# Reading K and V in 32 KB reads, written in 1 KB pieces to two partitions, in a decode kernel

## The chip, the cores and the metric

The kernel runs on one core of one Trainium2 chip. The metric is the device time of one execution in microseconds (us). "Span" is the profile's time from the first instruction to the last of one profiled execution; it is 1.7 to 1.9 us shorter than the device time. HBM is the chip's main memory, SBUF the core's own, of 128 partitions. A "packet" is one entry in the trace's record of DMA transfers; in these kernels it is one contiguous read.

## The reference

One decode step for 8 sequences: attention over the last 2,048 positions of a key and a value cache, plus an MLP, mixed by a sigmoid gate.

```python
# x: 8 x 1 x 576; k_cache, v_cache: 8 x 16 x 8192 x 128 (bf16); 32 query heads, 16 key heads
W = min(4096, max(256, Sk // 4))                       # 2048
q = (x @ wq).reshape(B, Sq, Hq, Dh).transpose(0, 2, 1, 3)
k = jnp.repeat(k_cache[:, :, Sk - W:, :], rep, axis=1)
v = jnp.repeat(v_cache[:, :, Sk - W:, :], rep, axis=1)
p = _softmax(jnp.einsum("bhqd,bhkd->bhqk", q, k) * Dh ** -0.5)
a = jnp.einsum("bhqk,bhkd->bhqd", p, v).transpose(0, 2, 1, 3).reshape(B, Sq, Hq * Dh) @ wo
b = ...                                                # layernorm, gelu MLP with w1, w2
return g * a + (1 - g) * b
```

What matters here: 2 x 8 x 16 x 2,048 x 128 x 2 bytes = 134 MB of K and V have to come out of HBM, of 154 MB in all.

## The kernel before

K and V come in 64 loads of 2 MB. (In the code and the views below, `arena` is the SBUF memory that all buffers lie in, `SE` a slot's 8,192 elements in one partition, 16 KB, and `AST` the step from one partition to the next.) A load takes one key head and four batches. Each lands in one of nine slots of 16 KB in each of the 128 partitions: partition 4x + a holds keys 64x to 64x + 63 of batch a, which are 16 KB in one piece in HBM. So a load is 128 reads of 16 KB, each written as one piece into one partition.

```python
def src_of(cache, g, q):
    hkv, b0 = 2 * g + q // 2, 4 * (q % 2)
    return cache[b0:b0 + 4, hkv, S0:Sk, :].rearrange("a (x r) d -> x a (r d)", x=32)
# ... in k_unit(i), and alike in v_unit(i):
s = take_slot()
d = dma("sp", lambda e: e.dma_start(slot(s), src_of(A_k_cache, g, q)), "s%d" % s, ...)
# K: VectorE transposes the slot, TensorE multiplies it with the queries; V: TensorE reads the slot
```

Another load matters to the argument: wo (four chunks of 1.2 MB) already goes through a helper that tells the DMA an order of writing of its own. It reads 4,608 bytes at a time and writes them in four pieces of 1,152 bytes into four neighbouring partitions.

```python
def run_dma(nc, e, out, in_, shape=None):       # shape: row pitch and (step, count) pairs, outermost first
    ...
# wo_chunk(i):
src = bass.AP(A_wo.tensor, offset=128 * h0 * D, ap=[[4 * D, 32], [128 * D, WO_CH], [1, 4 * D]])
run_dma(nc, e, dst[:, :, 0:D], src, (AST, ((4 * AST, 32), (WOP, WO_CH), (AST, 4), (1, D))))
```

All these loads are issued from the SP queue (SyncE's). The profile counts their packets together as q1, and their time as a share of the span of 16 DMA engines. That share is 98.6% in before, so the 16 are about equally loaded; the argument takes it that each load is spread evenly over them, gives each a queue of its own and numbers these e = 0 to 15.

## Time and profile before

| | before |
|---|---|
| time, median of 2 runs | 369.19 us (369.14 to 369.24) |
| span of the profiled run | 367.5 us |
| DMA packets' time, share of 16 engines' span | 98.6% |
| TensorE, VectorE busy | 69%, 57% |

First, three rows of the page of before: how busy the 16 DMA engines are in 40 equal slices of the span (9 is 90% or more), what they moved, and the queue that moves nearly all of it (packets, megabytes, share of 16 engines' span).

```profile
DMA  8999999999999999999999999999999999999994
GB/s 345 428 408 428 428 427 433 432 426 432 435 430 432 422 427 430 432 439 431 426 430 428 422 438 427 430 426 428 433 430 430 428 431 426 433 428 432 418 424 191
...
q1 hardware_dynamic: 11776, 154.29, 98.6%
```

The DMA engines are busy for 98.6% of the span, so the kernel's time is, within 5 us, the sum of its packets' times on one engine. That says what bounds it. The chain of waits of before agrees (shares of the span by what ended last):

```profile
DMA 74%; DVE 12%; PE 11%; SPq 1%; ACT 1%; issue 1%; DVEq 0%; ACTq 0%
```

The list of DMA issues shows how far ahead the loads are asked for (count, KB, median us from issue to landing). One load takes about 4.9 us, so some seven are waiting at any time.

```profile
arena<-in_A_k_cache_dram SPq DMA_DIRECT2D x32, 2048.0 KB, 35.8
arena<-in_A_v_cache_dram SPq DMA_DIRECT2D x32, 2048.0 KB, 36.7
```

Two stretches of the steady part (from the windows view of before: start and end, length, busy time and count for PE, PEld, DVE, ACT and POOL, granted TensorE clock, DMA share, GB/s; a share of 1.00 or 1.01 is full):

```profile
165.00:200.00 35.00, 24.01 (x152) 7.30 (x113) 24.32 (x27) 5.55 (x14) 3.79 (x18) 0.87 1.01 433
230.00:260.00 30.00, 20.32 (x117) 5.49 (x86) 20.72 (x26) 4.95 (x13) 1.89 (x9) 0.79 1.01 433
```

Since packets are everything here, the trace's record of each packet (size, start, duration) is the finest ruler. Counted over before, on queue q1 (its smaller packets, and 128 each of 3,456 and 4,096 bytes, left out):

```
bytes read   packets   median ns   what
     2,304       128          93   w2
     4,608     1,280         178   w1, wo (1,024 of them), w2
    10,368       384         389   w2
    16,384     8,192         611   K, V      (8,083 of them exactly 611)
    32,768       128       1,213   wq
    36,864       128       1,364   w1
```

A packet here is one read; how many pieces it is written in doesn't show in its count. The busy times of the engines and the durations of the 32 K-load issues on the SP queue (shortest, median and longest in ns, then first and last start in us):

```profile
PE 254.8 (69%) x1815; PEld 87.3 (24%) x1429; DVE 210.1 (57%) x253; ACT 47.8 (13%) x117; POOL 37.6 (10%) x163
L645 SPq DMA_DIRECT2D arena<-in_A_k_cache_dram x32: 534/535/1442, 2.6 to 282.9; - x32
```

### The profile page before, as it was taken

Reading aid. Unit: us, or ns where it says so; the run is one execution under the profiler, and the core shown is the slowest. Engines: PE = TensorE matmul, PEld = TensorE weight load, DVE = VectorE, ACT = ScalarE, POOL = GpSimd, SP = SyncE. Lnnn points to the kernel's source line nnn. Section 1 sums busy time; section 2 is a strip of 40 time slices with the busy share of each in tenths; the row PEclk is TensorE's granted clock in tenths of the full one; section 3 lists DMA queues with packets and bytes.
Section 4 is the critical chain, followed back from the end, with each engine's and each line's share of the span. In section 5 each row is a group of like instructions: output and inputs, shape, how many; then the busy total and the mean of one; then the engine's idle time right before and its main releaser. Section 6 shows DMA issues by size and latency. Waiting matters only on the chain.

```text
span 367.5 us, 4111 instructions
## 1 busy us (share of the span) xinstructions
PE 254.8 (69%) x1815; PEld 87.3 (24%) x1429; DVE 210.1 (57%) x253; ACT 47.8 (13%) x117; POOL 37.6 (10%) x163
## 2 busy tenths in 40 slices
PE   0349982895598398673986397765966396865995
PEld 0339200131123032010321032111311031214552
DVE  0704699797667754459654764478544864473000
ACT  1010002100300310003000300003100300003200
POOL 7020010011012001000101001010101000000000
PEclk9999998799689879887898879696988789795559
DMA  8999999999999999999999999999999999999994
GB/s 345 428 408 428 428 427 433 432 426 432 435 430 432 422 427 430 432 439 431 426 430 428 422 438 427 430 426 428 433 430 430 428 431 426 433 428 432 418 424 191
DMA packets 11851, 154.59 MB, mean 421 GB/s; under 512 B 1292, under 2 KB 1332, under 8 KB 3000
## 3 DMA queue, kind: packets, MB, share of 16 engines
q1 hardware_dynamic: 11776, 154.29, 98.6%
q8 instruction: 13, 0.21, 0.2%
q10 hardware_dynamic: 56, 0.03, 0.1%
q14 instruction: 6, 0.05, 0.0%
HBM read 154.31 MB, written 0.01 MB: 420 GB/s over the span
## 4 chain that ended last, share of the span: by engine, by line
DMA 74%; DVE 12%; PE 11%; SPq 1%; ACT 1%; issue 1%; DVEq 0%; ACTq 0%
DMA arena<-in_A_k_cache_dram 50%; DMA arena<-in_B_w_dram 15%; DMA arena<-in_A_v_cache_dram 9%; DVE arena L660 9%; PE ps L173 5%; PE ps L516 2%; PE ps L677 1%; DVE arena L605 1%; PE ps L700 1%; SPq L765 1%; ACT arena L619 1%; DVE arena L624 1%; PE ps L518 1%; PE ps L715 1%; DVE arena L614 0%
## 5 line engine op out<-in xcount | busy, mean ns | idle before, releaser
L660 DVE STREAM_TRANSPOSE arena<-arena 128x2048 f32<-128x2048 f32 x64 | 145.2, 2297 | 78.9 <-DMA arena<-in_A_k_cache_dram 71.5
L173 PE MATMUL ps<-arena 128*128 128x512 bf16 x401 | 134.4, 445 | 15.3 <-DVE arena L660 9.8
L677 PE MATMUL ps<-arena 128*128 128x512 bf16 x115 | 51.8, 450 | 16.7 <-DVE arena L660 16.6
L709 ACT ACTIVATE arena<-ps 128x512 f32<-128x512 f32 x32 | 19.1, 598 | 196.7 <-PE ps L700 196.7
L677 PEld LDWEIGHTS ps<-arena 128*128 128x128 bf16 x128 | 14.6, 114 | 125.8 <-issue 66.8
L715 PE MATMUL ps<-arena 128*128 128x8 f32 x256 | 36.9, 275 | 8.7 <-ACT arena L709 7.7
L653 POOL COPY arena<-arena 32x32 bf16<-32x32 bf16 x128 | 26.0, 203 | 159.2 <-PE ps L173 144.6
L715 PEld LDWEIGHTS ps<-arena 128*128 128x128 f32 x256 | 35.6, 217 | 22.4 <-ACT arena L709 16.4
L700 PE MATMUL ps<-arena 128*32 128x512 bf16 x512 | 36.7, 413 | 6.0 <-DMA arena<-in_A_v_cache_dram 6.0
L669 PE MATMUL ps<-arena 128*128 128x512 bf16 x6 | 3.5, 585 | 37.8 <-DVE arena L624 37.8
L605 DVE TENSOR_REDUCE arena<-ps 128x1 f32<-128x2048 f32 x8 | 18.3, 2282 | 15.5 <-PE ps L173 15.5
L619 ACT ACTIVATE arena<-ps,arena 128x512 bf16<-128x512 f32 x32 | 21.6, 686 | 41.4 <-DVE arena L614 41.4
L700 PEld LDWEIGHTS ps<-arena 128*32 128x32 bf16 x512 | 11.3, 100 | 39.8 <-issue 24.1
L624 DVE STREAM_TRANSPOSE arena<-arena 128x512 bf16<-128x512 bf16 x32 | 19.8, 674 | 0.9 <-ACT arena L619 0.9
L733 POOL TENSOR_TENSOR arena<-arena 128x16 bf16<-128x16 f32 x15 | 4.0, 267 | 142.3 <-ACT arena L725 142.3
L516 PE MATMUL ps<-arena 128*128 128x8 bf16 x144 | 10.9, 201 | 4.5 <-DMA arena<-in_B_w_dram 4.5
L559 PE MATMUL ps<-arena 128*8 128x288 bf16 (+1 forms) x140 | 11.6, 315 | 1.9 <-DMA arena<-in_B_w_dram 1.7
L516 PEld LDWEIGHTS ps<-arena 128*128 128x128 bf16 x144 | 10.8, 159 | 5.0 <-DMA arena<-in_B_w_dram 5.0
L669 PEld LDWEIGHTS ps<-arena 128*128 128x128 bf16 x8 | 0.9, 107 | 45.1 <-DVE arena L624 45.1
L733 DVE TENSOR_TENSOR arena<-ps,arena 128x16 bf16<-128x16 f32 x1 | 0.2, 229 | 19.4 <-PE ps L715 19.4
L438 PE MATMUL ps<-arena 8*128 8x8 bf16 x8 | 0.5, 168 | 13.5 <-DVE arena L411 9.8
L631 DVE RECIPROCAL arena<-ps 128x32 f32<-128x32 f32 x8 | 2.9, 358 | 10.5 <-PE ps L629 10.5
(83 smaller groups left out, 95.6 us busy)
## 6 DMA issues: line engine op xcount, KB each, us to landing
arena<-in_A_k_cache_dram SPq DMA_DIRECT2D x32, 2048.0 KB, 35.8
arena<-in_A_v_cache_dram SPq DMA_DIRECT2D x32, 2048.0 KB, 36.7
arena<-in_B_w_dram SPq DMA_DIRECT2D x1, 4608.0 KB, 24.3
arena<-in_A_wq_dram SPq DMA_DIRECT2D x1, 4096.0 KB, 13.1
arena<-in_B_w_dram SPq DMA_DIRECT2D x3, 1296.0 KB, 33.9
arena<-in_B_w_dram SPq DMA_DIRECT2D x2, 576.0 KB, 28.7
arena<-in_A_wq_dram SPq DMA_DIRECT2D x1, 512.0 KB, 3.7
arena<-in_B_w_dram SPq DMA_DIRECT2D x1, 432.0 KB, 30.4
```

What stands on the lines that cost most here:

```text
L173: return e.add_instruction(mybir.InstMatmult(name=nc.get_next_instruction_name(), engine=mybir.EngineType.PE, ins=[e.lower_ap(rhs), e.lowe ...
L516: ins = e.matmul(out_, lhsT, yT[:, kt, :], start=(kt == 0), stop=False)
L559: ins = e.matmul(ps[32 * j:32 * j + 8, BK_ACC, 0:JN], lhsT, rhs[:, JN * j:JN * j + JN], start=False, stop=True, skip_group_check=True, til ...
L605: mx = add("dve", lambda e: e.tensor_reduce(out=k(MX), in_=ps[:, 0:4, :].rearrange("p a n -> p (a n)"), axis=AXL.X, op=ALU.max), deps=[qk_ ...
L619: return e.activation(out=Pm[:, 512 * c:512 * c + 512], in_=ps[:, c, :], func=ACTF.Exp, bias=k(NB), scale=SCALE, accum_out=k(SUM + c))
L624: pts.append(add("dve", (lambda c=c: lambda e: e.transpose(bass.AP(arena, offset=aoffs("PT") + 2048 * (g % 2) + 128 * c, ap=[[AST, 128], [ ...
L653: return e.tensor_copy(dst, src)
L660: tr = add("dve", (lambda h=h, kb=kb: lambda e: e.transpose(bass.AP(arena_f, offset=foffs("KT") + kb * 2048, ap=[[AST // 2, 128], [1, 2048]]),
L677: mm = e.matmul(*args, start=False, stop=last) if rc == 0 else held_matmul(nc, e, *args, stop=last)
L700: mm = e.matmul(ps[c:c + 32, BK_OS[i % 2], :], PT[:, g % 2, 512 * q + 32 * t:512 * q + 32 * t + 32], slot(s)[:, 512 * t:512 * t + 512], st ...
L709: u_ev[i] = add("act", lambda e: e.activation(out=EV[:, i % 2, :], in_=ps[:, BK_OS[i % 2], :], func=ACTF.Copy), deps=[prev] + ([u_sum[i - ...
L715: mm = e.matmul(ps[:, BK_S, OC + 16 * (item % 2) + 8 * (q % 2):OC + 16 * (item % 2) + 8 * (q % 2) + 8], EV[:, i % 2, 128 * r:128 * r + 128 ...
```

## The change

The intent is fewer and larger reads: 32 KB, which is 128 keys of one batch. A slot has only 16 KB in a partition, so a read has to be written into two partitions; the change takes two that are 64 apart and alternates between them every 1 KB. Key block e is four reads of 32 KB, one for each batch, written to partitions 4e to 4e + 3 and 64 + 4e to 64 + 4e + 3. (That is how the program lays the transfer out; the author counts block e as queue e's, but the trace doesn't name a packet's engine or partition.) Which keys lie in which partition changes, alike for K and V, so the result doesn't.

```diff
-        def src_of(cache, g, q):
+        def load_quad(e, cache, g, q, s):
             hkv, b0 = 2 * g + q // 2, 4 * (q % 2)
-            return cache[b0:b0 + 4, hkv, S0:Sk, :].rearrange("a (x r) d -> x a (r d)", x=32)
+            blk = 2 * 64 * Dh
+            src = bass.AP(cache.tensor, offset=((b0 * Hkv + hkv) * Sk + S0) * Dh, ap=[[blk, 16], [Hkv * Sk * Dh, 4], [1, blk]])
+            piece = 4 * Dh
+            dst = bass.AP(arena, offset=aoffs("RAW") + s * SE, ap=[[AST, 128], [piece, SE // piece], [1, piece]])
+            return run_dma(nc, e, dst, src, (AST, ((4 * AST, 16), (AST, 4), (piece, SE // piece), (64 * AST, 2), (1, piece))))
...
-            d = dma("sp", lambda e: e.dma_start(slot(s), src_of(A_k_cache, g, q)), "s%d" % s, 4 * W * Dh * 2, ...)
+            d = dma("sp", lambda e: load_quad(e, A_k_cache, g, q, s), "s%d" % s, 4 * W * Dh * 2, ...)
...    (the same for A_v_cache)
```

No other instruction moves: the order and the waits on the four compute engines are those of before, line for line.

More of the change, by code (lines that the diff above doesn't have):

```diff
@@ L644, in k_unit @@
             s = take_slot()
-            d = dma("sp", lambda e: e.dma_start(slot(s), src_of(A_k_cache, g, q)), "s%d" % s, 4 * W * Dh * 2, deps=slot_free[s], name="dk%d" % i, after=last_dma[-1:])
+            d = dma("sp", lambda e: load_quad(e, A_k_cache, g, q, s), "s%d" % s, 4 * W * Dh * 2, deps=slot_free[s], name="dk%d" % i, after=last_dma[-1:])
             last_dma.append(d)
@@ L692, in v_unit @@
             item = 2 * g + q // 2
-            d = dma("sp", lambda e: e.dma_start(slot(s), src_of(A_v_cache, g, q)), "s%d" % s, 4 * W * Dh * 2, deps=slot_free[s], name="dv%d" % i, after=last_dma[-1:])
+            d = dma("sp", lambda e: load_quad(e, A_v_cache, g, q, s), "s%d" % s, 4 * W * Dh * 2, deps=slot_free[s], name="dv%d" % i, after=last_dma[-1:])
             last_dma.append(d)
```

## The prediction

> **What bounds the kernel.** The DMA engines. The row of DMA shares over the span has them 90% busy or more in 38 of 40 slices; the queue list puts 98.6% of 16 engines' span on the one SP queue, at 421 GB/s over all and 428 to 432 GB/s in the steady stretches (windows view). TensorE is 69% busy and VectorE 57%. The chain of waits is 74% DMA. K and V loads are issued about 36 us before they land, so some seven are queued and the queue never runs dry. The packets' own time sets the kernel's.
>
> **What a packet costs.** The trace's packet records: 16,384 B takes 611 ns in 8,083 of the 8,192 K/V packets; 36,864 B takes 1,364 ns, 32,768 B 1,213 ns (median, wq), 4,608 B 178, 2,304 B 93. These lie on one line: about 8.6 ns a packet + 0.03677 ns a byte (27.2 GB/s an engine). The records count packets by the reading side. The wo load, which reads 4,608 B and writes it in four pieces of 1,152 B into four partitions, shows 178 ns too in two thirds of its packets, about 194 in the rest (mean about 183).
>
> **What the change does.** Each of 64 loads has 64 reads of 32 KB instead of 128 reads of 16 KB: 4 packets an engine at about 1,213 ns instead of 8 at 611, 4,852 against 4,888 ns. That saves 36 ns a load, 64 x 36 = 2.3 us for each engine, all on the critical path. It adds write pieces: 2,048 of 1 KB a load, 128 an engine. Issuing them should cost little: the wo load, 1,024 write pieces, holds the SP queue for 0.71 us, a K/V load for 0.54; I estimate under 1 us a load, one every 4.9 us. Instruction order, waits, bytes, slots and compute are unchanged.
>
> **The risk.** [...] wo's mean of 183 instead of 178 ns says that split writes may cost 2 to 3%. That much on K/V (1,213 to about 1,243 ns) would make a load 4,972 ns: +5.4 us instead of -2.3.
>
> **Prediction.** 369.2 - 2.3 = 366.9; with a little for contention 367.1 us, 8 in 10 within 365.6 to 373.5. Faster by over 2%: 0.02; within 2%: 0.85; slower by over 2%: 0.13.
>
> **What would show it.** q1 packets fall by 64 x 64 = 4,096 to about 7,680; K/V packets of 32 KB at 1,213 ns; steady rate 431 to 435 GB/s; DMA share about 98%; engines' busy times unchanged. Contention would show as K/V packets above 1,220 ns with DMA share still near 100% and a lower GB/s. Starvation would show as a DMA share below 95% and long SP issues.
>
> **What would make it wrong.** [...] a limit on queued pieces that holds back issue, or 16 engines reading 32 KB blocks colliding in memory (wq's first packets took up to 1.5 us).

The sum came to 369.2 - 2.3 = 366.9 us, and the 0.2 us "for contention" that makes it 367.1 was an estimate, for which no measured number was given. The +5.4 us of the risk is 64 loads of 4,972 - 4,888 = 84 ns.

## The result and the profile after

| | before | after |
|---|---|---|
| time, median of 2 runs | 369.19 us | 389.79 us (389.51 to 390.08) |
| ratio, 95% interval | | 1.0558 (1.0513 to 1.0604) |
| span | 367.5 us | 388.2 us |
| DMA share | 98.6% | 98.5% |
| K/V packets, median | 8,192 of 611 ns | 4,096 of 1,285 ns |
| a load on one DMA engine | 8 x 611 = 4,888 ns | 4 x 1,285 = 5,140 ns |

A ratio is the mean time of one kernel's fast runs over that of the other's in the same rounds, so it can differ a little from the ratio of the medians.

The same rows of the page of after:

```profile
DMA  8999999999999999999999999999999999999995
GB/s 337 456 403 410 397 419 396 419 397 419 409 400 422 358 413 395 419 396 416 414 395 419 375 400 398 415 407 382 409 409 407 384 393 410 409 405 409 376 417 216
...
q1 hardware_dynamic: 7680, 154.29, 98.5%
```

The packets fell by 4,096, as the prediction said, and the engines are as busy as before. They move less at the same busy share: 404 and 407 GB/s in the two stretches below, against 433. So the packets themselves got longer. The same two stretches in the windows view of after:

```profile
165.00:200.00 35.00, 24.03 (x137) 6.85 (x96) 24.12 (x27) 4.94 (x13) 2.96 (x14) 0.85 1.00 404
230.00:260.00 30.00, 21.57 (x126) 4.92 (x89) 13.75 (x7) 1.56 (x4) 3.16 (x15) 0.83 1.00 407
```

Summing the packet records of q1 and dividing by 16 engines says where the time went:

```
us for each DMA engine   before   after   difference
K and V                   313.4   331.2        +17.8
wo                         11.7    14.0         +2.3
everything else            37.4    37.3         -0.1
sum                       362.5   382.5        +20.0
span less sum               5.0     5.7         +0.7
span                      367.5   388.2        +20.7
```

Of the 17.8 us, 64 x (5,140 - 4,888) ns = 16.1 us is the longer ordinary packet, and the rest is packets above the ordinary length, most of them near the wo chunks.

Something else in the profile after catches the eye more. The chain of waits of after, and a piece of the SP queue's timeline (start us, length us, what):

```profile
SPq 39%; DMA 27%; PE 17%; DVE 14%; issue 2%; ACT 0%; DVEq 0%; ACTq 0%
```

```profile
145.54 4.64 SPq L193 DMA_DIRECT2D arena<-in_A_v_cache_dram  x1
150.63 4.63 SPq L193 DMA_DIRECT2D arena<-in_A_k_cache_dram  x1
155.72 4.63 SPq L193 DMA_DIRECT2D arena<-in_A_v_cache_dram  x1
```

The engines' busy times, the durations of the K-load issues, and the loads' times from issue to landing (last figure, us) in after:

```profile
PE 265.0 (68%) x1815; PEld 88.9 (23%) x1429; DVE 210.2 (54%) x253; ACT 47.7 (12%) x117; POOL 37.5 (10%) x163
L193 SPq DMA_DIRECT2D arena<-in_A_k_cache_dram x32: 800/4634/24121, 2.8 to 323.8; - x32
arena<-in_A_k_cache_dram SPq DMA_DIRECT2D x32, 1.0 KB, 14.9
arena<-in_A_v_cache_dram SPq DMA_DIRECT2D x32, 1.0 KB, 15.0
```

Issuing one load now takes 4.63 us, where the prediction estimated under 1 us, and the issues form 39% of the chain. That looks like a cause: as if writing out 2,048 pieces took the queue 4.6 us. It isn't. The first K load of the same run, with only the wq and w1 loads queued before it, was issued in 0.80 us, and the second was then held for 24.12 us, until 2.6 us after the first packet of K had started. That fits an issue that waits for room: fewer loads are under way at a time (landing 15 us after issue, not 36, at about 5.1 us a load), the SP queue stands in front of them, and the chain of waits passes through it. The DMA share of 98.5%, against 98.6% before, says that the engines themselves hardly waited for it. Nor does the SP queue's share of the chain follow the loss: in the runs below it is 16% at a loss of 17.6 us and 28% at 3.0 us. The chain names what was released last; which resource was full is told by the busy share.

### The profile page after: what moved, and what is told of

Read it like the earlier page. It is cut to its first block, busy times and chain, and to the rows that moved or that the text cites. A ratio compares the mean times of both kernels' runs of the same rounds, so it can differ in the third digit from the quotient of the medians.

```text
span 388.2 us, 4175 instructions
## 1 busy us (share of the span) xinstructions
PE 265.0 (68%) x1815; PEld 88.9 (23%) x1429; DVE 210.2 (54%) x253; ACT 47.7 (12%) x117; POOL 37.5 (10%) x163
## 3 DMA queue, kind: packets, MB, share of 16 engines
q1 hardware_dynamic: 7680, 154.29, 98.5%
## 4 chain that ended last, share of the span: by engine, by line
SPq 39%; DMA 27%; PE 17%; DVE 14%; issue 2%; ACT 0%; DVEq 0%; ACTq 0%
SPq L193 39%; DMA arena<-in_A_k_cache_dram 23%; PE ps L173 9%; DVE arena L664 7%; DMA arena<-in_B_w_dram 4%; DVE arena L609 4%; PE ps L719 3%; PE ps L681 3%; PE ps L704 2%; DVE arena L628 1%; DVE arena L618 1%; DVE arena L612 1%; PE ps L673 0%; SPq L769 0%; PE ps L633 0%
## 5 line engine op out<-in xcount | busy, mean ns | idle before, releaser
L173 PE MATMUL ps<-arena 128*128 128x512 bf16 x401 | 140.5, 463 | 15.6 <-DVE arena L664 11.1
L681 PE MATMUL ps<-arena 128*128 128x512 bf16 x115 | 53.4, 465 | 23.9 <-DVE arena L664 23.9
L704 PE MATMUL ps<-arena 128*32 128x512 bf16 x512 | 38.0, 424 | 8.9 <-DMA arena<-in_A_v_cache_dram 8.9
L673 PE MATMUL ps<-arena 128*128 128x512 bf16 x6 | 3.5, 585 | 37.8 <-DVE arena L628 37.8
L559 PE MATMUL ps<-arena 128*8 128x288 bf16 (+1 forms) x140 | 13.1, 343 | 1.6 <-DMA arena<-in_B_w_dram 1.5
```

Source lines behind the costliest of these rows:

```text
L173: return e.add_instruction(mybir.InstMatmult(name=nc.get_next_instruction_name(), engine=mybir.EngineType.PE, ins=[e.lower_ap(rhs), e.lowe ...
L681: mm = e.matmul(*args, start=False, stop=last) if rc == 0 else held_matmul(nc, e, *args, stop=last)
L704: mm = e.matmul(ps[c:c + 32, BK_OS[i % 2], :], PT[:, g % 2, 512 * q + 32 * t:512 * q + 32 * t + 32], slot(s)[:, 512 * t:512 * t + 512], st ...
```

## The experiments

The theories at the start:

- **Theory 1, the piece:** every further write piece of a packet costs something, wherever it goes. From after: (1,285 - 1,213) / 31 = 2.3 ns.
- **Theory 2, sharing:** pairs of queues now write through something that they share (the texts call it a port) and get in each other's way, the more so the longer each stays in one half of its partitions. That any two queues share such a thing no trace or run here shows.
- **Theory 3, the switch:** going from one partition to another costs something, 31 times a packet.

A fourth, that 32 KB reads are slow by themselves, has against it that wq reads 32 KB at 1,213 ns in both kernels. All experiments but the last change only the function `load_quad`, and all that ran to the end gave the right result. The diffs are cut to what differs: from the change in the first 1 KB run, in the runs of halves and in the 4 KB alternating run, from the first 1 KB run in the two runs after it, and from the two pieces of 16 KB in the run with pairs 4 apart. Times are beside runs of before on the same chip (369.14 and 369.22 us).

### 1 KB pieces in the loads of before

The reads of before, one partition to a read, but 16 pieces to a packet.

```diff
+            src = cache[b0:b0 + 4, hkv, S0:Sk, :].rearrange("a (x r) d -> x a (r d)", x=32)
             piece = 4 * Dh
+            return run_dma(nc, e, dst, src, (AST, ((AST, 128), (piece, SE // piece), (1, piece))))
```

> The loads of before (16 KB reads, each landing in one partition, 128 partitions), but written in 1 KB pieces: the pieces of the change without its pairs of partitions and without its 32 KB reads. Theory 1: 611 + 15 x 2.3 = 646 ns a packet, 8 x 646 = 5168 ns a load, time about 387 us. Theories 2 and 3: 611 ns, 369 us (if the queues keep the partitions that they had).

Measured: 386.77 us (386.63 to 386.85), ratio 1.0475 (1.0459 to 1.0491); K/V packets 645 ns (median). Theory 1 said 646 ns and 387 us. Most of the loss of the change is here, 17.6 of 20.6 us, without a 32 KB read, without a pair of partitions, and with the packet count of before. Theories 2 and 3 expected 611 ns and 369 us. The queue line, the chain of waits and the two stretches of this run:

```profile
q1 hardware_dynamic: 11776, 154.29, 98.8%
DMA 34%; PE 25%; DVE 23%; SPq 16%; issue 2%; ACT 0%; DVEq 0%; ACTq 0%
```

```profile
165.00:200.00 35.00, 24.05 (x130) 6.05 (x89) 24.20 (x27) 4.76 (x12) 2.93 (x14) 0.82 1.01 407
230.00:260.00 30.00, 20.58 (x127) 4.94 (x92) 15.19 (x7) 1.97 (x4) 3.51 (x17) 0.89 1.01 407
```

The engines are full with 11,776 packets and move 407 GB/s, just as with 7,680 packets after the change: it is the pieces that count, not the packets.

### 4 KB pieces in the loads of before

```diff
-            piece = 4 * Dh
+            piece = 16 * Dh
```

> The loads of before in 4 KB write pieces, 4 to a packet. Theory 1 (each further write piece costs 2.27 ns, from 645 against 611 ns with 15 further pieces): 611 + 3 x 2.27 = 618 ns a packet, 8 x 7 ns x 64 loads = 3.5 us, time 372.7 us. If a few pieces a packet are hidden, as two thirds of the wo packets of before looked: 611 ns, 369.1 us.

Measured: 372.24 us, ratio 1.0087 (1.0072 to 1.0102); packets 616 ns (median). Theory 1 named 618 ns and 372.7 us. So few pieces aren't hidden, and cost nearly in proportion: three further pieces cost 5 ns (1.7 each), fifteen cost 34 ns (2.3 each). This run and the last differ in the piece size alone, and the author takes it that the queues share out the partitions alike in both (no trace shows it); and both go through the same helper, which by itself can then cost at most the 5 ns a packet. Here too the chain of waits has much of the SP queue in it, at a loss of 3 us that the packets account for: eight packets 5 ns longer, 64 times, are 2.6 us, and wo adds 0.4.

```profile
DMA 41%; SPq 28%; DVE 15%; PE 13%; issue 2%; ACT 0%; DVEq 0%; ACTq 0%
```

### 1 KB pieces in every fourth K and V load

```diff
+            if q != 3:
+                return e.dma_start(slot(s), src)
```

> The loads of before, with every fourth K and every fourth V load (16 of 64) in 1 KB pieces. Theory 1 with a fixed cost: these loads' packets 645 ns from first to last, 48 x 128 others 611; 16 x 8 x 34 ns = 4.4 us, time 373.5 us. [...] the first one to three packets of such a load at 611, the rest at 645 or more; time 371 to 373 us.

(The second case in it is that the first packets after large ones are cheap, as wo's 178 ns in before.)

Measured: 373.37 us, ratio 1.0113 (1.0097 to 1.0128). Of the 2,048 packets written in pieces 1,633 took 645 ns; about 26 of a load's 128, on average between one and two for each of 16 engines, were cheaper (613 to 636 ns in most). The time is what theory 1 with a fixed cost gives, 373.5 us; the few cheaper packets say that the first pieces after a stretch of large ones are partly free. Wo shows that better. Nothing was changed in wo, but:

```
wo's packets (1,024)                 at 178 ns   commonest lengths
before (one piece a K/V packet)         66%      178, 194, 198
4 KB pieces in K and V                   0%      186, 194, 180
1 KB pieces in K and V                   0%      186, 194, 185
```

In before, of a chunk's 256 packets the first 32 to start all take 178 ns in each of the four chunks, the last 32 hardly ever (0 to 19%). With pieces in front of it, wo pays from its first packets. This is what the prediction read wrongly: "178 ns too in two thirds of its packets" was not the price of a split write but the price of the first ones after large packets. Why they are cheaper no run here shows.

### Both halves one after the other, in 1 KB and in 16 KB pieces

The reads and the partitions of the change, but first the whole lower half and then the upper, in 32 pieces of 1 KB:

```diff
-(4 * AST, 16), (AST, 4), (piece, SE // piece), (64 * AST, 2), (1, piece)
+(4 * AST, 16), (AST, 4), (64 * AST, 2), (piece, SE // piece), (1, piece)
```

> Same reads, [...] same number of 1 KB write pieces as the change, but the sixteen pieces of the lower partition come first and then the sixteen of the upper, so the partition changes once in a packet, not 31 times. Theory 1 (each write piece after a packet's first costs (1285-1213)/31 = 2.3 ns, wherever it goes): packets stay at 1285 ns, time 390 us. Theory 2 [...]: packets of 1.3 to 2.4 us, time over 400 us. Theory 3 (each change of partition or port costs): packets near 1215 ns, time near 367 us.

and in two pieces of 16 KB:

```diff
-            piece = 4 * Dh
+            piece = SE
-(4 * AST, 16), (AST, 4), (piece, SE // piece), (64 * AST, 2), (1, piece)
+(4 * AST, 16), (AST, 4), (64 * AST, 2), (1, piece)
```

> 32 KB reads, two write pieces of 16 KB, lower partition and then upper. Theory 1: 1213 + 2.3 = 1215 ns a packet, time 367 to 368 us, a little faster than before. Theory 2: as for the run with halves in 1 KB pieces, [...] packets 1.3 to 2.4 us, time over 400 us. Theory 3: near 1215 ns, 367 us. If the packets stay at 1285 ns, neither pieces nor changes but the 32 KB reads are the cause.

Measured: 546.1 us (517.61 to 582.14) and 534.87 us (453.49 to 569.55). These kernels have no steady time of their own: their runs differ by 12% and 26%, so most of them count as slow by the rule of 1.5% above the fastest, and no ratio is formed. Before, in between on the same chip, stayed within 0.2%. The profiled runs counted as slow too, but the effect is far larger than a few per cent: K/V packets of 1,985 and 2,019 ns (medians), as against 1,285. The page of the second, with two pieces a packet:

```profile
DMA  9999999999999999999999999999999999999996
GB/s 379 408 252 262 259 259 244 257 249 260 258 252 251 242 277 252 256 249 256 250 258 253 260 287 285 284 287 277 286 288 280 284 286 279 269 286 272 289 311 276
...
q1 hardware_dynamic: 7680, 154.29, 99.1%
```

Theory 1 and theory 3 both expected 1,215 ns of this kernel, and the change's own loss would be gone; instead the rate falls to some 240 to 290 GB/s with full engines. That is what theory 2 expects where a packet stays on one side for long. The packet records of this run add a point that speaks for queues being in each other's way, and against a price of the 32 KB read or the pair of partitions by itself: the first K packet, started while other engines were still at w1, took 1,531 ns, the 33rd to the 64th about 2,050, the very last 1,532; and the quickest of all 4,096, 1,256 ns, ran in the middle of a wo chunk, with packets of wo started just before and after it. What they would share, this doesn't show. Theory 3 isn't needed: the 1 KB run in the loads of before never switched and paid 34 ns for 15 further pieces, 2.3 each, and at that price the 31 of the change are 70 of its 72 ns. Fewer switches made things worse, not better.

### 4 KB pieces, still alternating

```diff
-            piece = 4 * Dh
+            piece = 16 * Dh
```

> The change with 4 KB pieces, still alternating between partitions 64 apart. 8 pieces a packet. Theory 1 and theory 3 (both count pieces here): 1213 + 7 x 2.3 = 1229 ns, time 390 - 64 x 4 x 0.056 = 375 us less the rest, so 371 to 376 us. Theory 2: unchanged at about 1285 ns or worse, [...]; 388 us or more.

Measured: 435.89 us (425.68 to 446.18). K/V packets 1,501 ns. Eight pieces by theory 1 are 1,229 ns, so some 270 ns are something else, by theory 2 collisions. The order over 1 KB, 4 KB and 16 KB is 1,285, 1,501 and 2,019 ns: the longer a packet stays in one partition, the longer it takes. So the alternation every 1 KB in the change wasn't arbitrary: it escapes most of this loss, whatever its cause, and pays for it with pieces.

### Pairs of partitions 4 apart

The same two pieces of 16 KB, but key block e goes to partitions 8e to 8e + 7.

```diff
-(4 * AST, 16), (AST, 4), (64 * AST, 2), (1, piece)
+(8 * AST, 16), (AST, 4), (4 * AST, 2), (1, piece)
```

> 32 KB reads in two pieces of 16 KB as in the run that collided, [...] (the pair is 4 apart, not 64). [...] Theory 2[...]: packets of 1.8 to 2.1 us, time 450 to 570 us. If not the port but the distance of 64 partitions was the trouble: 1215 ns, 367.4 us, which would beat both kernels.

Measured: 569.5 us (512.5 to 574.31), K/V packets 1,979 ns. So it is not the distance of 64 alone that hurts: the packets are about as slow as with the pair 64 apart (2,019 ns). Theory 2 expected 1.8 to 2.1 us here; but the run doesn't prove it.

### A load in two DMAs of eight key blocks

Every load cut into two. The author meant each half to use eight of the 16 queues, so that no two would share; no run shows that it would.

> The run that collided most (32 KB reads, two pieces of 16 KB, 64 apart) with every load cut into two DMAs of 8 key blocks[...]. The time says nothing [...]; the packets do. Theory 2: 1213 + 2.3 = about 1215 ns, against 1.8 to 2.1 us with 16 queues. If the pair of partitions by itself were slow, packets stay above 1.8 us.

It gave nothing: the execution ended with a DMA abort. Why wasn't found. What it was to show, long pieces without sharing in packets of 32 KB, stays open. Theory 2 is the only one of the three whose expectations fit all the slow kernels, each time with the assumption that queues share something, and it stays unproven: no run isolated the sharing from the 32 KB reads and the pairs that all of those kernels have.

## Why the prediction was wrong

- **Right: what bounds the kernel, and that all of a packet's time counts.** The DMA share is 98.6% and 98.5%, and the packets' sum moved by 20.0 us of the span's 20.7.
- **Right: the packets, and nearly so the compute engines.** 7,680 packets on q1; VectorE 210.1 and 210.2 us busy. TensorE went from 254.8 to 265.0 us (264.6 in the 1 KB run); why wasn't looked into, and with full DMA engines nothing rests on it.
- **Not shown: the gain.** Two packets of 16 KB (1,222 ns) into one of 32 KB (1,213 ns as wq shows it) should be worth 64 x 36 ns = 2.3 us. The pieces hid it. In no version did the K/V reads reach 1,213 ns. A part can be seen at equal piece size: one read of 32 KB in 1 KB pieces takes 1,285 ns, two of 16 KB 2 x 645 = 1,290.
- **Wrong, and the step that failed: the price of the split writes.** The main sum gave them no price (packets of "about 1,213 ns"). For the bad case the prediction said "wo's mean of 183 instead of 178 ns says that split writes may cost 2 to 3%" and "That much on K/V (1,213 to about 1,243 ns)". They cost 72 ns a packet, 6%. Two errors lie in it. It scaled wo's surcharge with the packet's time, 3% of 4,608 bytes in four pieces carried over to 32,768 bytes in 32, where what grows is the number of pieces: three further pieces in one, 31 in the other. And it took the cheap first packets of a short burst for the lasting price; wo pays 186 ns as soon as pieces precede it. Mending the first error alone would have given the right sign: even wo's mean of 5 ns for three further pieces, counted by pieces, gives 31 x 1.7 = 52 ns a packet, 13 us in all against a gain of 2.3. With wo's lasting 8 ns (median) the sum would have been 31 x 2.7 = 83 ns.
- **Wrong: the cause of the risk.** It laid the surcharge of split writes on something that two queues share. In the loads of before the pieces cost the same 2.3 ns each with no pairs of partitions. What fits theory 2 is very dear where a packet stays long on one side (2,019 ns), but with alternation every 1 KB it is nearly absent from the steady packets, whose 72 ns the pieces explain but for 2. What else the change adds can be read beside the 1 KB run: K/V packets take 331.2 us for an engine with the change and 331.1 us there. That balance hides two things: the change's ordinary packets come to 5,140 ns a load against 8 x 645 = 5,160, 1.3 us less in all, and its longer ones to 1.4 us more. And wo takes 14.0 against 12.1 us. Why wo pays these 1.9 us more no run shows.
- **Wrong, but harmless: "I estimate under 1 us a load" for the issue.** It held for the first K load (0.80 us) and no other K load; their median was 4.63 us. The prediction had named "a limit on queued pieces that holds back issue" as a danger, and that fits what was measured. It made the load's lead shorter, 15 us for 36, with the DMA share at 98.5%.

## What to carry to other kernels

When DMA engines are full, count the write pieces of a transfer, not only the packets that the profile counts: here each further write piece cost about 2.3 ns, so 1 KB pieces took 5 to 6% of the bandwidth and 4 KB pieces under 1%. Where a packet is written into two partitions with 4 KB or more in one before the other, test it first: here all four such kernels lost far more (packets of 1,501 to 2,019 ns, against 1,285 at 1 KB; the cause unproven). And take the price of a small feature from a lasting stretch, never from the first packets of a short burst. A queue that takes 4.6 us to issue a load, and leads the chain of waits, cost next to nothing here, as the DMA engines behind it stayed full.
